# Three small loads move to the GpSimd queue, Wk's load follows at once, and the bias transposes move to the end of Q block 0

## Chip, core and metric

One NeuronCore of a Trainium2 chip. The time is the device time of one execution in microseconds (us). A kernel was run several times beside the kernel before on the same chip.

## The reference, cut to what matters

Sequence 2048, width 512, 32 heads of 16, bf16. The output mixes a sliding-window dilated attention (a) and a token-mixing MLP (b) by a gate:

```
g = sigmoid((x * gate_w).sum(-1))
a = attention(x @ wqkv) @ wo            # window 8, dilation 2
b = (gelu(layernorm(x)^T @ w1 + b1) @ w2 + b2)^T
out = g * a + (1 - g) * b
```

The change concerns only how the start is fed: x (2048 x 512), the Q and K parts of `wqkv` (Wq, Wk), and three tiny vectors `gate_w` (1 KB), `b1` (3.5 KB) and `b2` (4 KB), which are loaded as rows and turned into columns by TensorE transposes.

## The kernel before

The kernel describes its operations with the tiles that they read and write. A list scheduler with its own durations fixes each engine's order when the program is built, and derives the semaphore waits. TensorE's order is chained by hand, except for two groups of logit matmuls, which the scheduler places.

```python
for k_ in (0, 2):                  # x tiles 0..3 and Wq in four parts, 128 KB each
    xq(k_, "sp"); xq(k_ + 1, "act")
    wqq(k_, "sp"); wqq(k_ + 1, "act")
load("gw", GWR, ...)               # 4 rows of 256 B, SyncE queue
load("b1", B1R, ...)               # 14 rows
load("b2", B2R, ...)               # 16 rows
load("wk", ...)                    # 512 KB
ld_w("wv", ...)                    # 512 KB
for k_ in range(1, 4):
    ld_x(4 * k_, 4)                # 512 KB
    ld_xt(k_)                      # the same block by transposing DMA
# ... cut ...
def pe_q0(hb, dt): ...  # hb 0/1: left/right 256 columns, 2: all 512; 4 matmuls each
def f_tb(e):            # three tiny transposes into bank 4 (of TensorE's output memory): b1, gate_w, b2

pe_tx(0); pe_tx(1)      # x tiles 0 and 1: 8 transposes of 128x128 (L571)
PE(f_fill(2), ...)
pe_q0(0, 0)             # L592
pe_tx(2); pe_tx(3)      # x tiles 2 and 3 (L571)
pe_q0(0, 1)
PE(f_tb, 0.17, ["b1r", "b2r", "gwr", "ident"], ["b4"], "t_b12")   # L606 to L608
# ... VectorE copies gwrep, b1c, b2c ...
pe_q0(1, 0); pe_q0(1, 1)
pe_q0(2, 2); pe_q0(2, 3)
# then 44 groups of projections (L659), which start with K
```

## Time and profile before

| | before |
|---|---|
| time, three runs | 165.66, 165.93, 166.41 us |
| profiled run | 165.79 us, span 164.1 us |
| first K projection matmul | 9.73 us |

Two parts of the page: busy time of each engine, and the chain of work that ended last.

```profile
PE 159.4 (97%) x792; PEld 77.0 (47%) x808; DVE 150.7 (92%) x126; ACT 75.4 (46%) x104; POOL 11.9 (7%) x35
...
PE 93%; DMA 2%; SPq 1%; ACT 1%; issue 1%
```

TensorE (PE) is the bound. The same chain in order of time (start, duration, what) shows where it leaves TensorE:

```profile
3.44 3.20 DMA arena<-in_B_b_dram
6.64 0.14 issue
6.78 0.16 PE ps L606
...
6.99 1.64 PE ps L592 x11
8.63 0.05 issue
8.69 1.03 PE ps L592 x4
9.71 0.02 issue
9.73 9.88 PE ps L659 x45
```

Up to 6.78 us the chain runs through SyncE's issues and the landing of b2 (6.64 us); after that it is TensorE alone. TensorE's own instructions in that stretch, from the timeline (start, duration, group, count):

```profile
5.12 0.63 PE L592 MATMUL ps<-arena 128*128 128x256 bf16 x4
5.59 0.61 PE L571 MATMUL ps<-arena 128*128 128x128 bf16 x8
6.04 0.60 PE L592 MATMUL ps<-arena 128*128 128x256 bf16 x4
6.78 0.16 PE L606 MATMUL ps<-arena 14*128 14x14 bf16 x1
...
6.92 2.79 PE L592 MATMUL ps<-arena 128*128 128x256 bf16 x15
9.73 1.46 PE L659 MATMUL ps<-arena 128*128 128x512 bf16 x6
```

The four matmuls at 6.04 us are started by 6.36 us, yet the transposes begin only at 6.78 us. Busy time by engine in three slices (from:to and length, PE, PEld, DVE, ACT, POOL, granted clock, DMA share, GB/s):

```profile
4.00:5.00 1.00, 1.00 (x9) 0.68 (x7) 0.52 (x2) 0.61 (x2) 0.00 (x0) 1.00 1.06 368
5.00:6.00 1.00, 0.98 (x13) 0.87 (x13) 0.07 (x1) 0.16 (x1) 0.00 (x0) 1.00 0.90 126
6.00:7.00 1.00, 0.86 (x12) 0.60 (x10) 0.99 (x3) 0.66 (x2) 0.00 (x0) 1.00 0.84 272
```

Only 126 GB/s move between 5 and 6 us: a hole between the first eight loads and Wk, which was issued at 3.85 us and landed at 9.60 us. Landing times, here and below, are those of the last semaphore increment of a load in the trace.

### The profile page before, as it was taken

To read this page: it belongs to the slowest core of one execution; us is meant where nothing else is said; L and a number is where in the kernel's file an instruction comes from. 1 tells how busy PE (TensorE), PEld (TensorE's weight loads), DVE (VectorE), ACT (ScalarE), POOL (GpSimd) and SP (SyncE) were. 2 spreads that over 40 slices of the span, in tenths; PEclk is the share of its full clock that TensorE was granted. 3 is DMA by queue.
4 is the path that set the end of the run, shared out by engine and by line. 5 is a ranking of instruction groups with operands and counts; after the bars stand their busy time and mean duration, and the time that the engine had idled before them with its cause. 6 is when DMAs were issued, how large, how long until landed. Compare 5 with 4: busy or idle time off the path is not lost.

```text
span 164.1 us, 1991 instructions
## 1 busy us (share of the span) xinstructions
PE 159.4 (97%) x792; PEld 77.0 (47%) x808; DVE 150.7 (92%) x126; ACT 75.4 (46%) x104; POOL 11.9 (7%) x35
## 2 busy tenths in 40 slices
PE   7999999999999999999999999999999999999993
PEld 3745555555544444444444344444444444444641
DVE  0679999999999999999999999999999999999950
ACT  3356677666773699953211669210121111111164
POOL 3000030020000000005000000005000222000000
PEclk9999999999999999999999999999999999999999
DMA  4999999919499287999998994993996899981014
GB/s 153 284 240 249 258 178 252 185 22 188 92 310 290 50 230 202 291 290 259 158 205 245 278 250 145 295 242 113 280 226 177 164 205 184 211 201 36 32 57 135
DMA packets 44668, 32.24 MB, mean 197 GB/s; under 512 B 7924, under 2 KB 42228, under 8 KB 44660
## 3 DMA queue, kind: packets, MB, share of 16 engines
q1 hardware_dynamic: 41428, 22.06, 51.8%
q0 software_dynamic: 2512, 9.44, 28.9%
q10 hardware_dynamic: 720, 0.62, 1.1%
q8 instruction: 6, 0.10, 0.2%
q14 instruction: 2, 0.02, 0.0%
HBM read 18.88 MB, written 2.10 MB: 128 GB/s over the span
## 4 chain that ended last, share of the span: by engine, by line
PE 93%; DMA 2%; SPq 1%; ACT 1%; issue 1%
PE ps L857 29%; PE ps L884 29%; PE ps L659 23%; PE ps L893 8%; DMA arena<-in_B_b_dram 2%; PE ps L592 2%; SPq L491 1%; PE ps L721 1%; ACT arena L452 1%; PE ps L716 1%; PE ps L606 0%; PE ps L608 0%; PE ps L607 0%
## 5 line engine op out<-in xcount | busy, mean ns | idle before, releaser
L449 DVE TENSOR_TENSOR arena<-arena 128x4096 bf16<-128x4096 bf16 (+8 forms) x79 | 131.9, 1718 | 1.3 <-ACT arena L452 0.4
L884 PE MATMUL ps<-arena 128*128 128x512 bf16 (+2 forms) x234 | 50.0, 366 | 0.2
L857 PE MATMUL ps<-arena 128*128 128x512 bf16 x218 | 48.5, 379 | 0.3
L452 ACT ACTIVATE arena<-ps,arena 128x512 bf16<-128x512 f32 (+1 forms) x30 | 21.8, 732 | 58.0 <-PE ps L893 40.5
L452 ACT ACTIVATE arena<-ps 128x512 bf16<-128x512 f32 (+3 forms) x53 | 33.1, 629 | 18.4 <-PE ps L659 10.9
L659 PE MATMUL ps<-arena 128*128 128x512 bf16 x173 | 38.0, 379 | 0.2
L884 PEld LDWEIGHTS ps<-arena 128*128 128x128 bf16 x238 | 22.8, 98 | 25.9
L857 PEld LDWEIGHTS ps<-arena 128*128 128x128 bf16 x224 | 21.7, 98 | 26.9 <-ACT arena L452 0.7
L659 PEld LDWEIGHTS ps<-arena 128*128 128x128 bf16 x176 | 19.8, 113 | 18.3 <-DVE arena L691 0.5
L893 PE MATMUL ps<-arena 128*128 128x512 bf16 (+2 forms) x66 | 15.5, 366 | 0.1
L953 ACT ACT_TABLE_LOAD x11 | 14.1, 1283 | 2.9 <-issue 2.7
L691 DVE BATCH_NORM_STATS2 arena<-arena 128x6 f32<-128x512 bf16 x16 | 10.0, 679 | 0.7 <-DMA arena<-in_A_x_dram 0.6
L452 ACT ACTIVATE arena<-arena 128x16 f32<-128x16 f32 (+5 forms) x10 | 6.8, 679 | 7.3 <-DVE arena L449 7.0
L893 PEld LDWEIGHTS ps<-arena 128*128 128x128 bf16 x68 | 6.5, 98 | 7.3
L789 POOL DMA_DIRECT2D arena<-arena x8 | 4.3, 561 | 73.9 <-DVE arena L449 73.9
L705 DVE TENSOR_SCALAR arena<-arena 128x512 bf16<-128x512 bf16 x16 | 5.3, 402 | 0.0
L826 POOL DMA_DIRECT2D arena<-arena x3 | 3.6, 1210 | 18.9 <-DVE arena L449 18.9
L746 POOL DMA_DIRECT2D arena<-arena x2 | 2.5, 1268 | 31.4 <-DVE arena L449 31.4
L583 DVE COPY arena<-ps 128x256 bf16<-128x256 bf16 x4 | 1.1, 292 | 3.7 <-PE ps L571 3.6
L592 PE MATMUL ps<-arena 128*128 128x256 bf16 (+1 forms) x23 | 4.0, 307 | 0.1
L933 DVE TENSOR_SCALAR arena<-ps,arena 128x128 bf16<-128x128 f32 x1 | 0.4, 408 | 3.5 <-PE ps L893 3.5
L546 PE MATMUL ps<-const-bfloat16-1.0 128*128 128x512 bf16 (+1 forms) x9 | 2.7, 486 | 0.9 <-PEq L1003 0.9
(35 smaller groups left out, 17.5 us busy)
## 6 DMA issues: line engine op xcount, KB each, us to landing
arena<-in_B_w_dram SPq DMA_DIRECT2D x7, 1024.0 KB, 7.6
arena<-in_B_w_dram SPq DMA_DIRECT2D x8, 896.0 KB, 8.5
arena<-arena POOLq DMA_DIRECT2D x5, 1024.0 KB, 9.8
arena<-arena POOLq DMA_DIRECT2D x8, 512.0 KB, 11.1
out_dram<-arena SPq DMA_DIRECT2D x15, 128.0 KB, 1.7
arena<-in_A_x_dram SPq DMA_DIRECT2D x3, 512.0 KB, 4.9
arena<-in_A_wqkv_dram SPq DMA_DIRECT2D x2, 512.0 KB, 6.2
arena<-in_A_wo_dram SPq DMA_DIRECT2D x1, 512.0 KB, 8.3
```

Source lines behind the costliest of these rows:

```text
L449: return lambda e: e.tensor_tensor(out=o_, in0=a_, in1=b_, op=op_)
L452: return lambda e: e.activation(out=o_, in_=i_, func=f_, **kw)
L592: ins = e.matmul(ps[:, dl, c0:c1], lhsT=sub(WQKV, dt * 3 * D + dl, [(4, 128)]), rhs=XT[:, dt, c0:c1], start=(dt == 0 and hb == 0), stop=(d ...
L659: ins = e.matmul(ps[:, bank, :], lhsT=sub(WQKV, dt * 3 * D + tn * D + dl, [(4, 128)]), rhs=XT[:, dt, sb * 512:(sb + 1) * 512], start=(dt = ...
L691: A("dve", (lambda t_: lambda e: e.bn_stats(out=ST6[:, t_, :], in_=X[:, t_, :]))(t), 0.67, reads=["x%d" % t], writes=["st%d" % t], name="s ...
L705: A("dve", (lambda t_: lambda e: e.tensor_scalar(out=X[:, t_, :], in0=X[:, t_, :], scalar1=col(RSTD, t_), scalar2=col(NMR, t_), op0=ALU.mu ...
L789: prev = sch.dma("pool", (lambda d_, s_: lambda e: e.dma_start(d_, s_))(dst, src), 524288, sch.dsem("av%d_%d" % (h, c)), issue=1.0, reads= ...
L826: sch.dma("pool", (lambda o_, i_: lambda e: e.dma_start(o_, i_, accum_op=ALU.add, max_dma_last_dim=4096))(pw(0, 4), pw(4, 4)), 1800000, sc ...
L857: ins = e.matmul(ps[:, bank, :], lhsT=W1H[ft // 2][:, st, 128 * (ft % 2):128 * (ft % 2) + 128], rhs=X[:, st, :], start=(st == 0), stop=(st ...
L884: ins = e.matmul(ps[:, bank, 0:c1 - c0], lhsT=W2S[i // 2][:, ft, 128 * (i % 2):128 * (i % 2) + 128], rhs=UT[:, ft, c0:c1], start=(ft == 0) ...
L893: ins = e.matmul(ps[:, bank, 0:c1 - c0], lhsT=OT[:, i // 2, dl, 128 * (i % 2):128 * (i % 2) + 128], rhs=WO[:, dl, c0:c1], start=False, sto ...
L953: e.preload_act_table_set(want)
```

## The change

Its intent: take the three small issues off SyncE so that Wk is issued 1.2 us sooner, and put the transposes where their data has surely landed. Step (2,2) of Q block 0 becomes two halves, (0,2) and (1,2), so that TensorE has work to do before it needs the right half of x.

```diff
-load("gw", ..., issue=0.4)
-load("b1", ..., issue=0.4)
-load("b2", ..., issue=0.4)
 load("wk", ...)
+load("gw", ..., issue=0.6, queue="pool")
+load("b1", ..., issue=0.6, queue="pool")
+load("b2", ..., issue=0.6, queue="pool")
 ...
 pe_q0(0, 1)
-PE(f_tb, ..., ["b4"], "t_b12")        # and its three VectorE copies
+pe_q0(0, 2)
 pe_q0(1, 0)
 pe_q0(1, 1)
-pe_q0(2, 2)
+pe_q0(1, 2)
+PE(f_tb, ..., ["b7"], "t_b12")        # and its three VectorE copies, bank 7
 pe_q0(2, 3)
```

## The prediction

> **What bounds it now.** TensorE. The page gives PE 97% busy; the chain of waits lies 93% on PE, and from 9.73 us (first K projection) to 160.6 us it has no hole over 0.05 us. Granted clock: full. The change touches only the head before 9.73 us, so it can gain only there, and the 150 us behind should slide forward unchanged.
>
> **The head (timeline, landings).** SyncE issues its four x/Wq loads until 2.62 us, then gate, b1, b2 (0.37 + two of 0.34 us, with gaps), then Wk at 3.85 us. The first eight loads stop moving data at about 5.4 us; the DMA share falls to 0.35 in 5.5 to 6.0 us; Wk's packets start at about 6.0 us and it lands at 9.60 us. b2 lands at 6.64 us. On PE, step (0,1) of Q block 0 is issued out at about 6.49 us; the transposes wait for b2 and start at 6.78 us, the next step at 6.92 us. Q0 would be issued out at about 9.57 us (8 x 0.112 + 8 x 0.219 us after 6.92), but the first K weight load is at 9.70 us, after Wk's landing: a second wait, about 0.15 us.
>
> **What changes.**
> - SyncE loses three issues, 1.18 us, so Wk issues at about 2.67 us. The loads before it keep the DMA engines full until 5.4 us, so only the hole goes: I estimate that Wk lands 0.5 to 1.0 us earlier, 8.6 to 9.1 us.
> - GpSimd issues the small loads after the identity (1.38 us). Its 512 KB copies cost 0.56 us each to issue, so I estimate the third is out by 3.2 us and landed by 5.5 to 7 us. The Trainium skill, "DMA: Bandwidth & Descriptors", Specifications, gives about 1 us to first byte on this path against 0.6 us; no trace here shows it for so small a load. Needed at about 8.2 us now, so never waited for. The same page, "Issuing engines are not separate DMA queues", says that issuing from several engines saves only issue time: the gain is not bandwidth.
> - PE: the b2 wait (0.29 us) goes. Step (2,2) is split into (0,2) and (1,2): 8 x 0.112 instead of 4 x 0.219 us, +0.02 us. The transposes still cost 0.14 us.
>
> **Sum on the critical path.** Q0 ends at 9.57 - 0.29 + 0.02 = 9.30 us, with Wk already there: projections start 0.4 us sooner (9.73 to 9.3). Of Wk's 0.5 to 1.0 us only 0.15 counts.
>
> **Does the rest follow?** VectorE's last sum before the first logit matmul ends at 52.33 us, PE arrives at 53.06; the second 90.41 against 91.27; the last attention output 158.05 against about 159.7. Even if VectorE gained nothing, this slack covers 0.4 us.
>
> **Prediction.** 165.5 us, 165.0 to 166.2; before's runs spread over 0.75 us. Faster by over 2%: 1%. Within 2%: 98%. Slower by over 2%: 1%.
>
> **What would show it.** Wk issued near 2.7 us, landed before 9.1 us; no DMA hole at 5.5 to 6 us; no b2 in the chain; the first K matmul at 9.2 to 9.4 us; holes after it still 0.05 us; the small loads landed before 8 us.
>
> **What would make it wrong.** The small loads landing after 8.2 us; Wk's earlier packets delaying Wq's last blocks (landed 5.95 and 6.12 us, needed from 6.49 us); the instruction order, computed by a scheduler, placing logit matmuls before VectorE is done; Wk not landing earlier: no gain.

## More of the kernel before

The experiments came in three batches, on chip 4 (e1 to e4), chip 14 (r_before, r_after, e8, e9) and chip 11 (e1b, e5, e7, e8b).

## The result

| | before | changed |
|---|---|---|
| median of 6 runs | 166.06 us (165.64 to 166.41) | 165.88 us (165.60 to 166.17) |
| ratio | | 0.9992, 95% interval 0.9970 to 1.0014 |
| profiled run | 165.79 us | 165.92 us |

A ratio is the mean time of one kernel's runs over that of the other's in the same rounds, so it is not quite the ratio of the medians. Executions over 1.5% slower than the fastest of the same kernel are left out of the means. The time lies inside the predicted range, but the expected 0.4 us is not to be seen. The range, 165.0 to 166.2 us, also holds the median of the kernel before, so lying in it is no test of the 0.4 us. The same views of the changed kernel, first the page:

```profile
PE 160.6 (98%) x812; PEld 77.5 (47%) x812; DVE 150.7 (92%) x126; ACT 75.4 (46%) x104; POOL 13.7 (8%) x38
...
PE 94%; DMA 3%; ACT 1%; SPq 0%; issue 0%
```

The chain in order of time:

```profile
1.73 4.25 DMA arena<-in_A_x_dram
5.98 0.05 issue
6.03 0.66 PE ps L571 x8
6.68 2.18 PE ps L592 x20
8.87 0.11 PE ps L606
...
9.03 0.99 PE ps L592 x4
10.01 37.99 PE ps L660 x176
```

TensorE's timeline:

```profile
5.00 0.90 PE L592 MATMUL ps<-arena 128*128 128x256 bf16 x4
6.03 0.66 PE L571 MATMUL ps<-arena 128*128 128x128 bf16 x8
6.52 2.35 PE L592 MATMUL ps<-arena 128*128 128x256 bf16 x20
8.80 0.18 PE L606 MATMUL ps<-arena 14*128 14x14 bf16 x1
...
8.96 1.05 PE L592 MATMUL ps<-arena 128*128 128x512 bf16 x4
9.85 1.46 PE L660 MATMUL ps<-arena 128*128 128x512 bf16 x6
```

The slices from 4 to 6 us:

```profile
4.00:5.00 1.00, 1.00 (x8) 0.56 (x7) 0.58 (x2) 0.73 (x2) 0.04 (x1) 1.00 0.86 212
5.00:6.00 1.00, 0.90 (x5) 0.44 (x4) 0.00 (x0) 0.04 (x1) 0.00 (x0) 1.00 0.95 304
```

The intended effects are there: b2 is out of the chain, the DMA hole is filled (304 against 126 GB/s), Wk landed at 8.33 us. (The slice ahead of it lost about as much, 212 against 368 GB/s, so from 2 to 6 us hardly more was moved than before, 274 against 271 GB/s. e3 below, with the old loads, shows the same pair, 221 and 315 GB/s, so a full slice alone does not show an early Wk.) But a new link leads the chain: **the load of x tile 2**. Tile 2 landed at 5.98 us and tile 3 at 6.17 us; before it had been 5.19 and 5.38 us. The transposes of tiles 2 and 3 start at 6.03 instead of 5.59 us, and what the head saves later is gone before it begins. Three theories:

- **A**: the small loads on the GpSimd queue slow the x and Wq loads.
- **B**: Wk's earlier issue slows them.
- **C**: they land up to 0.8 us apart from run to run whatever the kernel, and the one profile of before was a lucky one.

### The profile page after: what moved, and what is told of

It reads as the page before. It is cut to its first block, busy times and chain, and to the rows that moved or that the text cites. A ratio compares the mean times of both kernels' runs of the same rounds, so it can differ in the third digit from the quotient of the medians.

```text
span 164.2 us, 2012 instructions
## 1 busy us (share of the span) xinstructions
PE 160.6 (98%) x812; PEld 77.5 (47%) x812; DVE 150.7 (92%) x126; ACT 75.4 (46%) x104; POOL 13.7 (8%) x38
## 4 chain that ended last, share of the span: by engine, by line
PE 94%; DMA 3%; ACT 1%; SPq 0%; issue 0%
PE ps L858 30%; PE ps L885 29%; PE ps L660 23%; PE ps L894 8%; DMA arena<-in_A_x_dram 3%; PE ps L592 2%; PE ps L722 1%; ACT arena L452 1%; PE ps L717 1%; SPq L491 0%; PE ps L571 0%; PE ps L606 0%; PE ps L608 0%; PE ps L607 0%
```

## The experiments

In the edits "after" means the changed kernel. Where an edit moves the model's clock, the scheduler may reorder engines far away, so most variants carry order constraints that pin the order, named with each (e1b, e5 and e7 have those of e1; e7 pins one VectorE product as well).

### e1: no loads on GpSimd

```diff
 load("wk", ...)
-three small loads on queue="pool"
 ld_w("wv", ...)
+three small loads on SyncE
 ...
-PE(f_tb, ...)  before pe_q0(2, 3), bank 7
+PE(f_tb, ...)  after the first four K projections, bank 3
+logit matmul groups pinned to their place among the MLP matmuls
```

> The changed kernel without its GpSimd loads: Wk and Wv follow the x and Wq loads on SyncE at once, the three small loads come after Wv on SyncE, and the bias transposes come after the first four K projections (bank 3). Place of the two groups of logit matmuls pinned as before. Theory A (the small loads on the GpSimd queue slow the x and Wq loads): x3 lands by 5.5 us as in the kernel before (5.38), against 6.17 in the changed kernel; Wk lands by 9.0 us; the first K projection matmul starts at 9.1 to 9.3 us (before 9.73, changed 9.85); time about 0.5 us under before, ratio 0.996 to 0.998. Theory B (Wk's earlier packets slow the x and Wq loads): x3 lands at 6.0 us or later, first K matmul at 9.6 us or later, time equal to before.

Measured: ratio 0.9990 (0.9966 to 1.0014), median 165.87 us. In the profiled run (165.34 us) tile 3 landed at 5.54, Wk at 8.85, the first K matmul started at 8.99 us. The profile looked like theory A, but the other five runs were 165.8 to 166.2 us: one profile doesn't decide.

### e2: GpSimd loads kept, Wk late

```diff
+three small loads on SyncE as well, into unused space, ahead of Wk
 load("wk", ...)
```

> The changed kernel with the small loads issued twice: on GpSimd as changed, and once more on SyncE between Wq and Wk, into unused space, so that Wk is issued as late as in the kernel before (about 3.9 us). Theory A: x2 and x3 land late all the same, x3 at 6.0 us or later. Theory B: x3 lands by 5.5 us.

Measured: 166.32 us (one run). Wk was issued at 3.88 us; tile 3 landed at 6.56 us all the same. So Wk's early issue is not needed for a late x (against B).

### e3: old loads, new TensorE order, order not pinned

```diff
-wk; three small loads on queue="pool"
+three small loads on SyncE; wk
```

> The changed TensorE order with the loads as in the kernel before (small loads on SyncE ahead of Wk, none on GpSimd). Both theories: x3 lands by 5.5 us, Q0 is issued out by about 9.3 to 9.45 us, but Wk lands near 9.6 us, so the first K matmul starts at 9.65 to 9.8 us, and the time equals that of before within 0.1%. If Wk did not matter, the K matmul would start at 9.5 us or sooner.

Measured: the four fast runs have the ratio 1.0066 (1.0017 to 1.0115), 165.51 to 167.78 us; the other two, 168.40 and 170.21 us, count as slow, and the profile is of the slowest. Its head is usable. Tile 3 landed at 6.02 us **with exactly the loads of before and none on GpSimd**, where theories A and B allow no lateness: the first support for C. Wk landed at 9.96 us and TensorE waited for it (Q0 issued out at about 9.70 us, first K matmul at 10.01 us). Its length has another cause, seen on TensorE's timeline, and on the page's line of the granted clock (tenths, 40 slices of 4.2 us):

```profile
23.63 1.24 PE L660 MATMUL ps<-arena 128*128 128x512 bf16 x5
27.13 1.24 PE L660 MATMUL ps<-arena 128*128 128x512 bf16 x5 [2.26 <-DMA arena<-in_A_x_dram]
...
PEclk9999998799999999999999999999999999999999
```

TensorE stood for 2.26 us waiting for the last transposing load of x, which took 9.8 us to land instead of 6.0 us in before. After that wait the clock fell as well: the trace's clock events give half clock from 28.32 to 31.73 us, and there 512-column matmuls followed each other at 427 instead of 216 ns. From start to start the wait cost 2.42 us and the half clock some 1.71 us (an estimate: half of 3.41 us), together 4.13 us, which is all that time - K (explained below the table) is above 156.07 us here (160.20 us). The scheduler had moved one VectorE product ahead, and so the first accumulating copy on GpSimd began at 18.91 us instead of 21.64 us, while that load was under way. That the copy slowed the load is argued from these times, not isolated. The 1.0066 is a fault of the experiment and tells nothing about the change; e8 repeats it pinned.

### e4: GpSimd loads held back

```diff
-three small loads on queue="pool"
+the same, waiting for ACT's copy of the last transposed x tile
+PE(f_tb, ...) after the first four K projections; logit groups pinned
```

> The changed kernel with the three GpSimd loads held back until ACT has copied the last transposed x tile (about 6.7 us), so after the x and Wq loads have landed; bias transposes after the first four K projections. Theory A (collision in time): x3 lands by 5.5 us, first K matmul at 9.1 to 9.3 us unless the small loads now delay Wk beyond 9.1 us; time 0.3 to 0.6 us under before. Theory B: x3 at 6.0 us or later, first K matmul at 9.6 us or later.

Measured: ratio 1.0063 (1.0037 to 1.0089), slower. Tile 3 landed at 6.07 us although GpSimd issued no load before 7.54 us: again late without A. The loss is a new wait: the small loads, issued at 7.54 to 8.78 us, landed at 14.08 to 14.52 us, 5.7 to 6.5 us each, behind the megabytes of weights and x then in flight, and TensorE stood for them (its timeline):

```profile
14.65 0.16 PE L603 MATMUL ps<-arena 14*128 14x14 bf16 x1 [1.36 <-DMA arena<-in_B_b_dram]
```

### r_before and r_after: both kernels once more

No edit.

> The kernel before, unchanged, once more: how much its head scatters. So far the time of a run less the start of its first K projection matmul was 156.06, 156.07 and 156.07 us (before, changed, e2), so each run's time tells where its projections began. Theory C (the x and Wq loads land up to 0.8 us apart from run to run whatever the kernel, and the one profile of before was a lucky one): x3 lands anywhere from 5.3 to 6.2 us in this profile, times from 165.4 to 166.6, mean near 166.0, so a mean K start near 9.95 us and not 9.73. Theory A (small GpSimd loads slow x and Wq): x3 lands by 5.6 us here as in the first profile.

> The changed kernel once more. Theory C: x3 lands anywhere from 5.4 to 6.3 us; mean time 0.1 to 0.45 us under before with the larger count of runs. Theory A: x3 lands at 6.0 us or later again.

Measured: r_before 0.9987 (0.9961 to 1.0013) against the other runs of **the same kernel**: this is what a ratio of two equal kernels looks like here. r_after 0.9988 (0.9964 to 1.0012) over five runs; its sixth, 168.20 us, was not profiled. In r_before tile 3 landed at 6.07 us, about as late as in the changed kernel (6.17 us). Theory C holds for the scatter, and theory A in the form "late only because of the GpSimd loads" falls. The chip is not the reason either: on chip 14 alone tile 3 landed at 6.07 us (r_before, r_after), 5.54 us (e8) and 5.47 us (e9). TensorE in r_before:

```profile
4.81 1.04 PE L592 MATMUL ps<-arena 128*128 128x256 bf16 x4
5.88 1.00 PE L571 MATMUL ps<-arena 128*128 128x128 bf16 x8
6.71 0.61 PE L592 MATMUL ps<-arena 128*128 128x256 bf16 x4
7.28 0.16 PE L606 MATMUL ps<-arena 14*128 14x14 bf16 x1
...
10.06 1.24 PE L659 MATMUL ps<-arena 128*128 128x512 bf16 x5
```

Compare with the first profile of before: the same eight transposes took 1.00 us instead of 0.61 us, and the four matmuls before them 1.04 instead of 0.63 us. Start to start, a 128-column transpose takes 107 ns here and 56 ns there, a 256-column matmul 213 and 109 ns: TensorE ran at half its rate until 6.7 us, in the first profile only until about 5 us. The clock column of the slices reads 1.00 all through, because it counts time without a recorded clock event as full. The packed trace of the first profile holds such an event, full clock from 4.91 us; that of r_before holds none. And b2, which landed at 7.15 us, was hardly waited for: the transposes start 0.23 us after the last matmul of step (0,1), where without any wait it is 0.20 us.

### e8 and e8b: new TensorE order with the old loads, pinned

```diff
-wk; three small loads on queue="pool"
+three small loads on SyncE; wk
+TensorE, VectorE and ACT pinned to the order of after
```

> Half the change: the changed TensorE order (bias transposes between the last two steps, Q0 step 2 in halves) with the loads as before. Order of every engine pinned to that of the changed kernel, unlike in e3, where one VectorE product was moved ahead. The b2 wait is gone but Wk still lands late: all theories, K start waits for Wk by 0.1 us or more; mean time within 0.15 us of before. Times above 167 as in e3 must not come back, and no wait of TensorE for an x load between 20 and 30 us.

> e8 once more, for the count. In the ten profiles so far, the first K matmul starts 3.39 us after the last transpose of x tiles 2 and 3 wherever the changed TensorE order ran without another wait (changed kernel, its repeat, e2, e8), 3.46 to 4.22 us with the old order. Here: 3.39 us unless Wk is waited for. If the first e8 was no luck, its mean time is again 0.2 us or more under before, with before's runs near 166.1; if it was luck, the mean of both is within 0.15 us of before.

Measured: 0.9969 (0.9945 to 0.9994) and 0.9994 (0.9977 to 1.0012). The times of e3 did not come back. The first K matmul started at 9.23 and 9.99 us; tile 3 had landed at 5.54 and 6.30 us. Wk, issued late as in before, landed at 8.43 and 9.14 us and was not waited for, against the expectation of a wait of 0.1 us or more. The repeat fits neither branch of its expectation: it is 0.1 us under before, both together 0.3 us.

### e9: new loads with the old TensorE order, pinned

```diff
-three small loads on SyncE; wk        (in before)
+wk; three small loads on queue="pool"
+TensorE, VectorE and ACT pinned to the order of before
```

> The other half: the loads as changed (small loads on GpSimd, Wk at once), TensorE order as before, every engine pinned to the order of before. The bias transposes stand right after step (0,1) and wait for b2. Wk no longer bounds. Theory C: b2 lands 6.1 to 6.8 us, about as late after x3 as before, so the b2 wait stays and K starts 0 to 0.2 us sooner than before: mean time 0 to 0.2 us under before. Theory A: x3 late by 0.5 us, mean time 0.2 us or more over before.

Measured: 1.0027 (1.0004 to 1.0050), slower. TensorE:

```profile
5.82 0.71 PE L571 MATMUL ps<-arena 128*128 128x128 bf16 x8
6.37 0.60 PE L592 MATMUL ps<-arena 128*128 128x256 bf16 x4
7.76 0.16 PE L606 MATMUL ps<-arena 14*128 14x14 bf16 x1 [0.79 <-DMA arena<-in_B_b_dram]
...
10.53 0.81 PE L659 MATMUL ps<-arena 128*128 128x512 bf16 x3
```

Tile 3 came early (5.47 us), but b2 landed at 7.63 us, and the transposes, in their old place, waited for it. Both expectations missed the cause: what the new loads delay visibly is the small loads themselves. b2 took 3.8 to 5.3 us from issue to landing in the five profiles where GpSimd issued it among the first loads (changed kernel, r_after, e2, e5, e9), against 3.2 to 4.0 us in the five where SyncE issued it at 3.4 us (before, r_before, e3, e8, e8b). Whether GpSimd's queue does this, or Wk, whose packets in the new loads no longer come after b2, is not separated. The 3.8 us is e2's, the one of the five in which Wk is issued late, and from SyncE behind Wk and Wv b2 took 6.1 us (e1): both speak for Wk.

### e1b, e5 and e7: 0, 3 and 6 loads on GpSimd

```diff
 e1b = e1
 e5  = e1 with the three small loads on queue="pool" after wk
 e7  = e5 with the three loads issued twice (first into unused space)
```

> e1 once more: Wk at once, no GpSimd loads, transposes after the first K projections; the zero of the series of 0, 3 and 6 GpSimd loads. Mean time again 165.7 to 165.95 us; the first K matmul 3.10 us after the last transpose of tiles 2 and 3.

> e1 with the three small loads on GpSimd, as the change has them, and all else as e1. Theory A (they slow the x and Wq loads): 0.2 to 0.4 us slower than e1 in the mean, x3 at 6.0 us or later. Theory B (Wk issued early slows them) and theory C (scatter alone): the mean of e1 within 0.15 us.

> e5 with the three small loads issued twice on GpSimd, the first time into unused space. Theory A: twice the loss of e5 against e1, 0.4 to 0.8 us, and x3 or the Wq loads later than in any run so far without them. Theories B and C: the mean of e1 within 0.15 us.

Measured: e1b 0.9975 (0.9957 to 0.9993), e5 1.0005 (0.9968 to 1.0042), e7 0.9989 (0.9976 to 1.0002). In means: e1 and e1b 165.86 us over twelve runs (e1b, on the chip of the other two, 165.88 us), e5 165.98 us over five and 168.05 us in the sixth, e7 166.06 us over five. Theory A expected e7 0.4 to 0.8 us over e1; it is 0.2 us, and e5 without its odd run 0.1 us. A cost of that size for the GpSimd loads is not excluded, but not shown either. The landings say the same: tile 3 came at 5.90 us in the mean of the eight profiles without early GpSimd loads and at 6.18 us in the mean of the six with them, while within each group it scatters with a standard deviation of 0.4 us. (e1b missed its expected 3.10 us of K - E by 0.12 us: the third part of Wq landed at 7.12 us, and step (0,2) waited for it.) The odd run of e5 is the profiled one:

```profile
6.40 1.03 PE L571 MATMUL ps<-arena 128*128 128x128 bf16 x8 [0.36 <-DMA arena<-in_A_x_dram]
7.22 3.96 PE L592 MATMUL ps<-arena 128*128 128x256 bf16 x21
```

Here TensorE stayed at half rate until 10.0 us; the 256-column steps until then followed each other at 213 instead of 109 ns. In the table below, K - E is 4.55 instead of 3.10 us and E is 0.56 us later than in e7: together 2.0 us, the whole excess over e7's 166.00 us. Its listing bears no mark of slowness (granted clock 1.00), since the time before the first clock event counts as full; that event, full clock, comes at 10.07 us. Why so late is open.

### All heads side by side

Of each profile: landing of x tile 3, of b2 and of Wk, start of the last transpose of tiles 2 and 3 (E), start of the first K matmul (K), in us. In e1, e1b, e4, e5 and e7 the bias transposes come after K, so b2 is no part of K.

| | x tile 3 | b2 | Wk | E | K | K - E | time - K |
|---|---|---|---|---|---|---|---|
| before | 5.38 | 6.64 | 9.60 | 5.98 | 9.73 | 3.75 | 156.06 |
| r_before | 6.07 | 7.15 | 9.22 | 6.60 | 10.06 | 3.46 | 156.05 |
| e9 (new loads, old order) | 5.47 | 7.63 | 8.74 | 6.32 | 10.54 | 4.22 | 156.07 |
| changed | 6.17 | 6.75 | 8.33 | 6.47 | 9.85 | 3.39 | 156.07 |
| r_after | 6.07 | 7.54 | 8.95 | 6.68 | 10.07 | 3.39 | 156.09 |
| e8 (old loads, new order) | 5.54 | 6.63 | 8.43 | 5.84 | 9.23 | 3.39 | 156.05 |
| e8b (the same) | 6.30 | 7.44 | 9.14 | 6.60 | 9.99 | 3.39 | 156.08 |
| e2 | 6.56 | 6.52 | 9.07 | 6.86 | 10.25 | 3.39 | 156.07 |
| e3 | 6.02 | 7.11 | 9.96 | 6.32 | 10.01 | 3.69 | not used |
| e1 | 5.54 | | 8.85 | 5.89 | 8.99 | 3.10 | 156.35 |
| e1b | 6.29 | | 8.67 | 6.59 | 9.81 | 3.22 | 156.39 |
| e4 | 6.07 | | 9.38 | 6.58 | 9.68 | 3.10 | 157.76 |
| e7 | 6.26 | | 8.10 | 6.56 | 9.66 | 3.10 | 156.34 |
| e5 | 6.54 | | 9.28 | 7.12 | 11.67 | 4.55 | 156.38 |

Three readings follow.

1. *time - K* is 156.05 to 156.09 us in all eight usable profiles with the transposes ahead of K. Whatever the head gives, the rest hands on undiminished. Nothing was given back behind the head.
2. *K - E* is 3.39 us in all five profiles of the new TensorE order in which Wk was not waited for (e3 waits for Wk), with old loads and new. In the old order it is 3.46 to 4.22 us. This is where the change works: in the first profile 3.75 - 3.39 = 0.36 us, in the repeat of before 3.46 - 3.39 = 0.07 us. Even of the 0.07 us, some 0.06 us is not the change's: step (0,1) began at half rate there, and from E to its last matmul took 0.45 instead of 0.38 us.
3. *E* lies anywhere from 5.84 to 7.12 us. It follows tile 3 by 0.30 us where TensorE had its full rate and was waiting for the tile, and by 0.5 us or more in most profiles where it was still at half rate. So two things scatter in it: the landing, and the time at which TensorE comes to its full rate.

## Why the prediction was right, and where its sum was not

**Right: the bound, and that the rest slides.** Reading 1 shows it to 0.04 us.

**Right: Wk and the DMA hole.** Wk was issued at 2.67 us, landed at 8.33 us (8.95 in the repeat; predicted 8.6 to 9.1), and the slice of the hole was filled, though e3's was too. Over all profiles Wk landed at 8.79 us in the mean of the eight that issue it at 2.7 us, and at 9.24 us in the mean of the six that issue it at 3.9 us: 0.45 us earlier for 1.2 us of issue (predicted 0.5 to 1.0). The risk that the prediction named, late last parts of Wq, did not bite: they landed at 6.72 and 6.91 us and the first was needed at 6.96 us.

**Right: b2 no longer waited for.** It landed at 6.75 and 7.54 us (predicted 5.5 to 7) and was needed at 8.8 and 9.0 us. The new loads need the new order: alone they were 0.27% slower (e9), where b2 landed later than the old place of the transposes can bear. The new order alone (e8, e8b) lost nothing.

**Mis-sized: the b2 wait, predicted 0.29 us.** From the last matmul ahead of the transposes to the first transpose it is 0.41 us in the first profile and 0.20 us where nothing is waited for. So the wait was 0.21 us there, and 0.03 us in the repeat (0.23 us). What I took for wait was in part the transposes' own cost. That cost, predicted 0.14 us, is 0.29 us: K - E is 3.39 us with them and 3.10 us without. It cancels, since both orders pay it.

**Mis-sized: the Wk wait, predicted 0.15 us.** 0.18 us in the first profile and 0.31 us in e3, but none in r_before, e8 and e8b, which all have the late Wk issue. On most heads Wk's earlier landing is worth nothing.

**The step that failed: "Q0 ends at 9.57 - 0.29 + 0.02 = 9.30 us".** It put the change on top of one profile's head, as if that head were fixed. K was predicted at 9.2 to 9.4 us and came at 9.85 us, because E came 0.49 us later. That lateness is shown to be possible without the new loads (r_before, with nothing changed; e3, e8b). And 9.73 us was an early K: by reading 1, the mean of the kernel before over its 45 runs, 166.11 us, puts its K at about 10.05 us (an estimate), and the mean of the changed kernel's eleven fast runs, 165.94 us, at about 9.87 us. Both waits that the change removes are differences of landing times that scatter, so the gain is not a constant: 0.36 us where tile 3 came early and both waits occurred, at most 0.07 us in r_before, where tile 3 and slow transposes were late enough to cover b2, and Wk came 0.38 us earlier.

**So the answer to "where did the gain go".** A constant 0.4 us was never there to gain. Measured against before in the same rounds the changed kernel gained 0.08% and 0.12% (0.13 and 0.20 us), no more than a repeat of before against itself (0.13%). The intervals reach 0.9970 and 0.9964, so the times alone do not exclude 0.4 us (0.24%); the two profiles of before, 0.36 and at most 0.07 us, say that it was there only at times. Why the landings scatter was not examined. Still open is whether the GpSimd loads delay the x loads, at a cost of 0.1 to 0.2 us; e5 and e7 point that way, within the scatter. e8 and e1, which keep the small loads off GpSimd, had ratios of 0.9969 and 0.9994, 0.9990 and 0.9975. They may be better than before by some 0.3 us; with one interval of two reaching 1 for each, and 0.9987 for before against itself, this is not established.

The prediction cited the Trainium skill, "DMA: Bandwidth & Descriptors", for the first byte on GpSimd's path (Specifications), which no run here isolates, and for the statement that several issuing engines save only issue time ("Issuing engines are not separate DMA queues"). The trace agrees with the second: 1.2 us of issue time was saved, and DMA bandwidth was no higher where the engines were busy (344 to 383 GB/s between 7 and 10 us in before, 350 to 378 GB/s in the changed kernel).

## What to carry to other kernels

A wait at the start of a kernel is the difference of two times that scatter, so take several profiles of the kernel before, and cost a removed wait by its spread, not by one reading. Subtract a fixed point (here the first K matmul) from the total of each profile: if the rest is constant, every run's time tells where its head ended. When loads are reordered, see which of them then lands later, and move its consumer with it, and check each experiment for instructions that a scheduler has moved elsewhere.

## What the Trainium skill lacked or had wrong

- "TensorE: Matmul & The Clock Gate", Part 1, has the half-rate start right: 107 and 56 ns per 128-column step, as it states. It says that the transition comes about 4 us into sustained activity, within 500 ns. Counted from the first matmul at 0.85 us, it came here after at most 2.7 us (e2), and after about 3.0 us (e8), 4.8 us (changed kernel), 5.8 us (r_after) and 9.2 us (e5), with short waits of TensorE for loads in between.
- The same page, Part 4, says that the full rate doesn't engage for transposes. Here the eight transposes of x tiles 2 and 3 followed each other at 56 ns in the first profile of before and at 107 ns in r_before: they ran at either rate. (The trace records them as matmuls and does not show whether they use the page's transpose mode.)
- The same page warns under "Seeing it yourself" that the recorded clock events are not to be fully trusted. That agrees only in part: three of the fourteen profiles (r_before, r_after, e2) hold no clock events, but in the other eleven the first event lies where the matmuls change from slow to fast steps, as at 10.07 us in e5.
- "DMA: Bandwidth & Descriptors", "Anatomy of one DMA — SWDGE (gpsimd) path", fits about 2.0 us plus bytes over bandwidth to a DMA from GpSimd. For 1 to 4 KB behind other loads it was 3.8 to 5.3 us for b2 among the first loads, and 5.7 to 6.5 us in e4.
- No page that I read tells how far the landing of a load scatters from run to run. For 128 KB issued at 1.73 to 1.74 us (x tile 3) it was 5.38 to 6.56 us over fourteen profiles, enough to hide a gain of 0.4 us.
